# DMA time in a list schedule: a softmax attention and token-mixing MLP kernel planned again with DMA prices, finer DMA keys and measured GpSimd times

## The chip, the cores and the metric

The kernel runs on one core of one Trainium2 chip. The metric is device time in microseconds (us) of the whole program; each quoted time is the median of three to seven runs. A profile shows one further view, the span from first to last instruction, which is about 2 us shorter than the timed run. The core has TensorE (PE, matmuls), VectorE (DVE), ScalarE (ACT), GpSimd (POOL) and SyncE, whose sequencer (SPq) issues nearly all DMAs here. Every run also gives the mean granted clock of TensorE; that clock is either 1.0 or 0.5 at any moment, so a mean clock c over a span means 2 × (1 − c) × span microseconds "at half clock".

## The reference, cut to what matters

```python
x  = A_x                                 # 2048 x 512, bf16
xn = layernorm(x)
q, k, v = split(xn @ wqkv)               # 32 heads of 16
p  = softmax(q k^T / 4)                  # 32 x 2048 x 2048 exponents
a  = (p v) @ wo
u  = gelu(layernorm(xn)^T w1 + b1)       # mixes tokens: 2048 -> 1376
y  = (u w2 + b2)^T                       # 1376 -> 2048
return x + a + y
```

The exponents dominate: 134 million of them, cut into 1024 tiles of 128 × 1024. One tile is two heads' scores for part of the keys. Most tiles go to ScalarE (one instruction each); some go to VectorE, which approximates the exponent by integer arithmetic on the bits in five instructions (`dW`, `dM`, `dA`, square, product), and whose result needs three second matmuls instead of one.

## The kernel before

The kernel is written as a *list schedule*. A Python class places one instruction after another on the engine where it can start soonest, by a price list, and keeps a modelled clock for each engine. The chip then executes each engine's list in order, waiting on semaphores. Prices decide the order only; data dependencies are found by keys that each instruction reads and writes, in the order in which the instructions are planned. So a wrong price should give no wrong result, as long as no buffer is planned to be filled again before its reader is planned. What a wrong price does is to put an instruction where its engine must stand and wait.

```python
EXP_I, EXP_L = 0.903, 1.03      # ScalarE exponent: issue, latency (us)
P1_I, P1_L = 1.13, 1.22         # VectorE: first step of an exponent tile
DMA_L = 2.2                     # DMA: issue to landing
D_GAP = 3                       # at least so many tiles between two on VectorE
D_BACKLOG = 1.2                 # and no more VectorE work than this waiting
...
def _time(self, op, cost, ready):
    if op.is_dma:
        op.t0 = max(self.free[eng], ready)
        self.free[eng] = op.t0 + 0.06          # issue price of a DMA
        op.t1 = op.t0 + cost[1]                # 2.2
...
def task_qt(qb, T):                            # queries of a pair of head blocks
    ...
    for e_ in range(2):
        slot = (8 * qb + 2 * T + e_) % 4
        for r in range(4):
            a = 32 * r + 16 * e_
            yield "sp", [dict(dst=QT[a:a + 16, slot, :], src=Qall[a:a + 16, :], reads=[("Qall",)],
                              writes=[("QT", slot)], name="q_row")]     # one key for four rows
...
def task_epilogue(b):                          # head block b: divide by the row sums
    yield "pvev", [... tensor_copy(OT32[:, eb, :], bank(PV_BANK)) ...]          # VectorE
    for r in range(4):
        yield "sp", [... dcomp <- OT32 ...]                # 4 DMAs: row sums, reshaped
    yield "dve", [... reciprocal(rcomp, dcomp) ...]        # waits for these 4
    yield "sp", [... rden_d <- rcomp ...]                  # 1 DMA to DRAM
    for r in range(4):
        yield "sp", [... denb <- rden_d, broadcast ...]    # 4 DMAs back
    yield "dve", [... oT = OT32 * denb ...]                # waits for these 4
...
# GpSimd: normalisation of a row block and V scaling, both priced 0.9 us
def ln2_norm(t):  sc.add("pool", ..., cost=(0.9, 1.0))
def vm_scale(tiles, T):  sc.add("pool", ..., cost=(0.9, 1.0))
```

DMA generators (`yield "sp"`) were emitted at once when their turn came. The kernel works through 32 head blocks (four heads and 512 queries each) of 32 exponent tiles each; where the text below speaks of "a head" of the plan, it means such a block. Beside them it fills TensorE's spare time with "filler" tasks on one more PSUM bank: K, V and query projections, the MLP's up-projection (`ut`), and the output tiles (`fin`). Filler is unevenly spread: blocks 1 to 12 have 100 to 268 filler matmuls, blocks 13 to 16 and 20 to 24 have 0 to 16.

The softmax here doesn't subtract the row's maximum and nothing guards it: scores larger than these inputs give would overflow.

Of the kernel before, what the change touches and what calls it, by code (L numbers as in the profile page):

```python
# [11 lines left out]
F32 = mybir.dt.float32  # L12
# [44 lines left out]
DMA_L = 2.2  # L57
D_GAP = 3
D_LAST = 28
D_BACKLOG = 1.2  # L60
# [23 lines left out]
class Sched:  # L84
# [43 lines left out]
    def _time(self, op, cost, ready):  # L128
        eng = op.eng
        if op.is_dma:  # L130
            op.t0 = max(self.free[eng], ready)
            self.free[eng] = op.t0 + 0.06
# [22 lines left out]
    def add(self, eng, fn, reads=(), writes=(), name="", dma=False, out_dma=False, cost=None):  # L155
# [3 lines left out]
        if cost is None:  # L159
            cost = (0.06, DMA_L) if dma else (("F", (0, 1, 2, 3), 0.22) if eng == "pe" else (EV_I, EV_L))  # L160
# [94 lines left out]
def bass_parallel_sum__softmax_full_mha__mixer_token_mlp__prompt_kernel(  # L255
# [18 lines left out]
    with ExitStack() as es:  # L274
# [42 lines left out]
        u_sb = sb("u_sb", [128, 512], F32)  # L317
        ga_sb = sb("ga_sb", [128, 512], F32)
# [57 lines left out]
        sc.add("pool", lambda e: e.memset(QT[:, 2:4, :], 0.0), writes=[("QT", 2), ("QT", 3)], cost=(0.8, 0.9))  # L376
# [38 lines left out]
        def late_consts():  # L415
            for half in range(2):
                sc.add("pool", lambda e, half=half: e.memset(wo_pad[:, 4 * half:4 * half + 4, :], 0.0),
                       writes=[("wo_pad", g) for g in range(4 * half, 4 * half + 4)], cost=(1.8, 1.9))
            for e_ in range(2):
                for r in range(4):  # L420
                    src = A_wo.rearrange("(T q) n -> q T n", q=128)[32 * r + 16 * e_:32 * r + 16 * e_ + 16, :, :]
                    dst = wo_pad[32 * r:32 * r + 16, :, :].rearrange("p (T e) n -> p T e n", e=2)[:, :, e_, :]
                    dma("sp", dst, src, reads=[], writes=[("wo_pad", g) for g in range(NG)], name="ld_wo")
# [30 lines left out]
        def ln2_norm(t):  # L454
            sc.add("pool", lambda e: e.tensor_scalar(xn_sb[:, t, :], xn_sb[:, t, :], mv[:, t, 3:4], None, ALU.mult),  # L455
                   reads=[("xn", t), ("mv", t)], writes=[("xn", t)], cost=(0.9, 1.0))
# [49 lines left out]
        def vm_scale(tiles, T):  # L506
# [4 lines left out]
                cost=(0.9, 1.0))  # L511
# [17 lines left out]
        def qt0_evac():  # L529
            sc.add("act", lambda e: e.activation(QT[:, 0, :], bank(EX_BANK), ACTF.Identity, scale=qmask[:, 0:1]),  # L530
                   reads=[("bank", EX_BANK), ("qmask",)], writes=[("QT", 0)], cost=(0.6, 0.69))
            sc.add("dve", lambda e: e.tensor_scalar(QT[:, 1, :], bank(EX_BANK), qmask[:, 1:2], None, ALU.mult),
                   reads=[("bank", EX_BANK), ("qmask",)], writes=[("QT", 1)])
# [51 lines left out]
        def score_specs(n):  # L585
# [3 lines left out]
            for i in range(2):  # L589
# [6 lines left out]
                    reads=[("KTt", T, kt), ("QT", b % 4)], writes=[("bank", bk)], name="sc",  # L596
# [102 lines left out]
        def task_qt(qb, T):  # L699
            for ct in range(NCT):  # L700
# [5 lines left out]
                              reads=[("bank", EX_BANK)], writes=[("Qall",)])]  # L706
            for e_ in range(2):
                slot = (8 * qb + 2 * T + e_) % 4
                for r in range(4):
                    a = 32 * r + 16 * e_  # L710
                    yield "sp", [dict(dst=QT[a:a + 16, slot, :], src=Qall[a:a + 16, :], reads=[("Qall",)],
                                      writes=[("QT", slot)], name="q_row")]
# [32 lines left out]
        def w1_load(ft):  # L745
# [3 lines left out]
                reads=[], writes=[("wblk", slot)], name="ld_w1")  # L749

        def w2_load(i):
# [3 lines left out]
                reads=[], writes=[("wblk", slot)], name="ld_w2a")  # L755
            dma("sp", wblk[0:FLAST, slot, NFT - 1, :], B_w2[128 * (NFT - 1):F, 128 * st:128 * (st + 1)],
                reads=[], writes=[("wblk", slot)], name="ld_w2b")
            dma("sp", wblk[FLAST:FLAST + 1, slot, NFT - 1, :],
                B_b2[128 * st:128 * (st + 1)].rearrange("(o j) -> o j", o=1),
                reads=[], writes=[("wblk", slot)], name="ld_b2")  # L760
# [3 lines left out]
        def task_ut(ft):  # L764
            slot = ft % NW
            m = min(128, F - 128 * ft)
            for st in range(NT):
                yield "pe", ext_mm(m, lambda a, z, st=st: wblk[:, slot, st, a:z], xn_sb[:, st, :],
                                   [("wblk", slot), ("h", st)], st == 0, st == NT - 1, "ut")
            if ft + NW < NFT:  # L770
                yield "call", lambda: w1_load(ft + NW)
            else:
                yield "call", lambda: w2_load((ft + NW - NFT + 1) % 2 if NFT % 2 else ft + NW - NFT)
            yield "ev", [dict(eng="dve", fn=lambda e: e.tensor_scalar(u_sb[0:m, :], bank(EX_BANK)[0:m, :],  # L774
                                                                      b1col[0:m, ft:ft + 1], None, ALU.add),
                              reads=[("bank", EX_BANK), ("b1col",)], writes=[("u",)])]
            yield "free", None
            yield "dve", [dict(eng="dve", fn=lambda e: e.scalar_tensor_tensor(
                ga_sb[0:m, :], u_sb[0:m, :], GELU_A, u_sb[0:m, :], ALU.mult, ALU.mult),
                reads=[("u",)], writes=[("ga",)])]  # L780
            yield "dve", [dict(eng="dve", fn=lambda e: e.scalar_tensor_tensor(
                ga_sb[0:m, :], ga_sb[0:m, :], 1.0, u_sb[0:m, :], ALU.add, ALU.mult),
                reads=[("ga",), ("u",)], writes=[("ga",)])]
            yield "act", [dict(eng="act", fn=lambda e: e.activation(ga_sb[0:m, :], ga_sb[0:m, :], ACTF.Tanh, scale=GELU_C),
                               reads=[("ga",)], writes=[("ga",)], cost=(0.5, 0.64))]
            yield "dve", [dict(eng="dve", fn=lambda e: e.scalar_tensor_tensor(
                gT(ft)[0:m, :], ga_sb[0:m, :], 1.0, u_sb[0:m, :], ALU.add, ALU.mult),
                reads=[("ga",), ("u",)], writes=[("gT", ft)] + (WKV_KEYS if ft < 8 else []))]

        def task_fin(i):  # L790
# [5 lines left out]
            for ft in range(NFT):  # L796
                k = 128 if ft < NFT - 1 else FLAST + 1
                yield "pe", ext_mm(128, lambda a, z, ft=ft, k=k: wblk[0:k, slot, ft, a:z], gT(ft)[0:k, :],
                                   [("wblk", slot), ("gT", ft)] + ([("gTone",)] if ft == NFT - 1 else []),
# [3 lines left out]
            for G in range(ng):  # L803
                yield "pe", ext_mm(128, lambda a, z, G=G: oT[:, qb % 2, G, 128 * sti + a:128 * sti + z], wo_pad[:, G, :],
                                   [("oTc", qb % 2, G), ("wo_pad", G)], False, G == ng - 1, "op")
# [5 lines left out]
            else:  # L811
# [3 lines left out]
                    reads=[("bank", EX_BANK), ("x", st)], writes=[("osb", ob)])]  # L815
                yield "sp", [dict(dst=out2[128 * st:128 * (st + 1), :], src=osb[:, ob, :], reads=[("osb", ob)],
# [4 lines left out]
        def task_epilogue(b):  # L821
            qb, G = divmod(b, NG)
            eb = b % 2
            yield "pvev", [dict(eng="dve", fn=lambda e: e.tensor_copy(OT32[:, eb, :], bank(PV_BANK)),  # L824
# [9 lines left out]
            for r in range(4):  # L834
                yield "sp", [dict(dst=denb[32 * r:32 * r + 16, eb, :],
                                  src=rden_d[eb:eb + 1, 512 * r:512 * (r + 1)].to_broadcast([16, 512]),
                                  reads=[("rden_d", eb)], writes=[("denb", eb, r)], name="den_out")]
# [64 lines left out]
        for j in range(4):  # L902
            vm_scale(list(range(4 * j, 4 * j + 4)), 0)
# [321 lines left out]
```

## Time and profile before

The median was 879.62 us of three runs (873.07 to 880.71).

| | before |
|---|---|
| busy share: TensorE / VectorE / ScalarE | 90% / 83% / 90% |
| exponent tiles on ScalarE / VectorE | 839 / 185 |
| start to start of two ScalarE exponents when nothing stalls | 0.90 us |
| VectorE waits for the row-sum DMAs and the broadcast DMAs | 24.8 + 10.1 us |
| mean granted clock | 0.939 |

The next fence holds lines of the profile's page of the kernel before: the busy sums; the busy tenths of TensorE and ScalarE in 40 equal slices with the granted clock in tenths under them; and the engines on the chain that ended last.

```profile
PE 787.1 (90%) x8124; PEld 229.7 (26%) x8124; DVE 730.6 (83%) x1227; ACT 792.9 (90%) x860; POOL 78.5 (9%) x90
...
PE   5985899899999998999799999989989999898994
...
ACT  4984799899999998999989999998999999899992
...
PEclk9998899999999998989958999995899999999998
...
DVE 35%; PE 34%; DMA 13%; ACT 7%; SPq 5%; POOL 5%; issue 2%; DVEq 0%
```

Three engines are nearly equally busy, and 18% of the chain of waits is DMA or the DMA queue, though all DMA engines together are hardly used (29 GB/s). The clock row dips to 5 where ScalarE dips too.

The next fence cuts the same execution into stretches (view by windows): before the first exponent; block 0; block 1; blocks 2 to 4; 5 to 12; 13 to 31; after the start of the last exponent (below just "after the last exponent"). Block borders are every 32nd exponent start, read from the trace. Columns: from:to, length, busy us (and count) of PE, weight loads, DVE, ACT, POOL; granted clock; DMA share; GB/s.

```profile
0.00:16.60 16.60, 7.43 (x67) 6.44 (x67) 9.07 (x28) 5.36 (x10) 9.04 (x31) 1.00 0.78 221
16.60:48.30 31.70, 27.97 (x273) 13.82 (x277) 22.65 (x70) 29.77 (x32) 16.40 (x26) 0.89 0.01 2
48.30:88.50 40.20, 27.98 (x424) 8.82 (x424) 27.35 (x40) 24.81 (x27) 37.04 (x26) 0.85 0.22 46
88.50:169.20 80.70, 72.71 (x1216) 26.50 (x1216) 72.48 (x114) 73.50 (x79) 15.97 (x9) 0.97 0.05 11
169.20:377.90 208.70, 198.29 (x2232) 54.62 (x2232) 181.10 (x297) 201.45 (x224) 0.00 (x0) 0.98 0.21 44
377.90:859.00 481.10, 445.37 (x3840) 116.91 (x3842) 409.11 (x666) 456.95 (x490) 0.00 (x0) 0.93 0.08 19
859.00:876.30 17.30, 7.31 (x88) 2.62 (x80) 8.85 (x15) 1.02 (x2) 0.00 (x0) 0.77 0.09 30
```

Block 1 took 40.2 us with ScalarE busy 27.9 of them. Nineteen blocks (13 to 31) took 481 us, 25.3 us each, at clock 0.93. A block whose 26 ScalarE tiles follow each other at 0.90 us would take 23.5 us.

Who waited for whom (columns: engine and line, releaser, us in all, times, longest), first the engines, then the DMA queue's own:

```profile
DVE dW L619 <- PE ps L592: 65.6, 55, 4.7
...
ACT pT L608 <- PE ps L592: 52.6, 65, 6.0
...
DVE rcomp L830 <- DMA dcomp<-OT: 24.8, 18, 3.4
...
PE ps L654 <- POOL VM L508: 12.7, 5, 5.9
...
DVE oT L838 <- DMA denb<-rden_scratch: 10.1, 11, 2.4
```

```profile
SPq L348 <- DMA QT<-Qall: 121.6, 90, 3.0
...
SPq L348 <- DMA wblk<-in_B_w_dram: 75.1, 32, 3.9
```

The DMA queue stood 121.6 us behind query rows: four rows shared one key, so each waited for the landing of the one before.

### The profile page before, as it was taken

How to read it: one execution, taken by the hardware profiler on the slowest of the kernel's cores; microseconds unless marked ns; L12 is line 12 of the kernel's file. 1: busy time of each engine (PE TensorE's matmuls, PEld its weight loads, DVE VectorE, ACT ScalarE, POOL GpSimd, SP SyncE). 2: the span in 40 equal slices, each digit the busy share in tenths (PEclk: the TensorE clock that was granted, in tenths of full speed). 3: DMA queues.
4: the chain of work that ended last, by engine and by line, in shares of the span. 5: the costliest groups of instructions: out<-in, count | busy, mean ns of one | idle time of the engine just before them, and what ended most of it. 6: DMA issues, size and time to landing. Idle time of an engine off the chain costs nothing.

```text
span 876.3 us, 19148 instructions
## 1 busy us (share of the span) xinstructions
PE 787.1 (90%) x8124; PEld 229.7 (26%) x8124; DVE 730.6 (83%) x1227; ACT 792.9 (90%) x860; POOL 78.5 (9%) x90
## 2 busy tenths in 40 slices
PE   5985899899999998999799999989989999898994
PEld 3522333222222221222212222221222222222221
DVE  6775898898998877887868889897998888798985
ACT  4984799899999998999989999998999999899992
POOL 5499121100000000000000000000000000000000
PEclk9998899999999998989958999995899999999998
DMA  5003000022132102100000111100000111100110
GB/s 168 1 23 59 14 9 16 6 59 56 31 62 46 44 15 52 47 14 10 13 6 8 36 30 24 38 15 5 10 12 6 32 25 34 37 15 8 24 25 25
DMA packets 73238, 25.36 MB, mean 29 GB/s; under 512 B 63104, under 2 KB 71168, under 8 KB 73152
## 3 DMA queue, kind: packets, MB, share of 16 engines
q1 hardware_dynamic: 69984, 22.57, 11.4%
q10 hardware_dynamic: 3168, 1.57, 0.6%
q8 instruction: 63, 1.03, 0.5%
q14 instruction: 23, 0.19, 0.1%
HBM read 19.54 MB, written 2.35 MB: 25 GB/s over the span
## 4 chain that ended last, share of the span: by engine, by line
DVE 35%; PE 34%; DMA 13%; ACT 7%; SPq 5%; POOL 5%; issue 2%; DVEq 0%
PE ps L592 13%; DVE dW L619 13%; PE ps L654 12%; PE ps L683 7%; ACT pT L608 7%; DVE dM L630 5%; SPq L348 5%; DVE dM L628 5%; DMA dcomp<-OT 4%; DVE dM L622 4%; POOL hx L455 3%; DMA wblk<-in_B_w_dram 3%; DVE dA L625 2%; DMA denb<-rden_scratch 2%; DMA rden_scratch<-rcomp 2%
## 5 line engine op out<-in xcount | busy, mean ns | idle before, releaser
L608 ACT ACTIVATE pT<-ps 128x1024 bf16<-128x1024 f32 x839 | 783.7, 1098 | 55.4 <-PE ps L592 52.6
L592 PE MATMUL ps<-QT,KT 32*128 32x512 bf16 x2048 | 348.2, 403 | 35.3 <-DVE dW L619 21.3
L619 DVE TENSOR_SCALAR dW<-ps 128x1024 int16<-128x1024 f32 x185 | 225.6, 1219 | 66.2 <-PE ps L592 65.6
L654 PE MATMUL ps<-pT,V 128*32 128x512 bf16 x1678 | 274.2, 407 | 5.3 <-DVE OT L824 3.5
L592 PEld LDWEIGHTS ps<-QT,KT 32*128 32x128 bf16 x2048 | 85.2, 91 | 348.4 <-ACT pT L608 127.4
L630 DVE TENSOR_TENSOR dM<-dW,dM 128x1024 bf16<-128x1024 bf16 x185 | 127.7, 691 | 2.8
L628 DVE TENSOR_TENSOR dM<-dM 128x1024 bf16<-128x1024 bf16 x185 | 128.5, 695 | 0.0
L654 PEld LDWEIGHTS ps<-pT,V 128*32 128x32 bf16 x1678 | 64.5, 95 | 114.6 <-issue 89.1
L654 PE MATMUL ps<-dM,VM 128*32 128x512 bf16 x370 | 74.8, 408 | 16.1 <-POOL VM L508 12.7
L622 DVE TENSOR_SCALAR dM<-dW 128x1024 int16<-128x1024 int16 x185 | 80.7, 436 | 3.1
L654 PE MATMUL ps<-dW,V 128*32 128x512 bf16 x370 | 75.4, 411 | 8.7 <-DVE OT L824 7.9
L625 DVE TENSOR_SCALAR dA<-dW 128x1024 int16<-128x1024 int16 x185 | 78.6, 425 | 0.0
L654 PE MATMUL ps<-dA,V 128*32 128x512 bf16 x370 | 73.6, 410 | 1.0 <-DVE V L740 0.5
L683 PE MATMUL ps<-hx,wblk 128*32 128x512 bf16 x688 | 57.8, 383 | 0.3 <-DVE u_sb L774 0.3
L683 PE MATMUL ps<-wkv_raw,wblk 128*32 128x512 bf16 x512 | 41.4, 383 | 1.8 <-DVE Qall L705 1.2
L683 PE MATMUL ps<-wo_pad,oT 128*32 128x512 bf16 x480 | 42.0, 392 | 0.0
L508 POOL TENSOR_SCALAR VM<-V 128x544 bf16<-128x544 bf16 x16 | 26.9, 1685 | 65.2 <-DVE V L740 62.3
L838 DVE TENSOR_TENSOR oT<-OT,denb 128x512 bf16<-128x512 f32 x31 | 21.3, 688 | 10.1 <-DMA denb<-rden_scratch 10.1
L830 DVE RECIPROCAL rcomp<-dcomp 128x16 f32<-128x16 f32 x31 | 7.8, 252 | 24.9 <-DMA dcomp<-OT 24.8
L654 PEld LDWEIGHTS ps<-dM,VM 128*32 128x32 bf16 x370 | 18.1, 96 | 38.7 <-issue 15.3
L455 POOL TENSOR_SCALAR hx<-hx,mv 128x512 bf16<-128x512 bf16 x16 | 26.7, 1684 | 0.1
L654 PEld LDWEIGHTS ps<-dW,V 128*32 128x32 bf16 x370 | 17.9, 95 | 32.2 <-issue 14.7
(79 smaller groups left out, 373.4 us busy)
## 6 DMA issues: line engine op xcount, KB each, us to landing
wblk<-in_B_w_dram SPq DMA_DIRECT2D x10, 512.0 KB, 4.4
wblk<-in_B_w_dram SPq DMA_DIRECT2D x16, 320.0 KB
denb<-rden_scratch SPq DMA_DIRECT2D x124, 32.0 KB, 1.8
out_dram<-osb SPq DMA_DIRECT2D x16, 128.0 KB, 1.8
dcomp<-OT SPq DMA_DIRECT2D x124, 2.0 KB, 1.7
QT<-Qall SPq DMA_DIRECT2D x120, 16.0 KB, 1.7
x_sb<-in_A_x_dram SPq DMA_DIRECT2D x3, 512.0 KB, 10.1
wkv_raw<-in_A_wqkv_dram ACTq DMA_DIRECT2D x2, 384.0 KB, 9.4
```

The lines of the kernel that those rows point to most:

```text
L348: return eng.dma_start(dst, src)
L455: sc.add("pool", lambda e: e.tensor_scalar(xn_sb[:, t, :], xn_sb[:, t, :], mv[:, t, 3:4], None, ALU.mult), reads=[("xn", t), ("mv", t)], w ...
L508: sc.add("pool", lambda e: e.tensor_scalar(vm_kh[:, t0_:t0_ + n, 8 * T:8 * T + 8, :], v17_kh[:, t0_:t0_ + n, 8 * T:8 * T + 8, :], CM, None ...
L592: specs.append(dict(eng="pe", fn=lambda e, r=r, bk=bk: e.matmul(bank(bk), lhsT=KT[32 * r:32 * r + 32, T, 128 * kt:128 * (kt + 1)], rhs=QT[ ...
L608: return [dict(eng="act", fn=lambda e: e.activation(pT[:, pbuf[n], :], ps[:, s_ * 1024:(s_ + 1) * 1024], ACTF.Exp, scale=LN2_128), reads=[ ...
L619: yield dict(eng="dve", fn=lambda e: e.tensor_scalar(dW_i[:, buf, :], ps[:, s_ * 1024:(s_ + 1) * 1024], IBIAS, 0.0, ALU.add, ALU.max), rea ...
L622: yield dict(eng="dve", fn=lambda e: e.tensor_scalar(dM_i[:, buf, :], dW_i[:, buf, :], 0x7f, 0x3f80, ALU.bitwise_and, ALU.bitwise_or), rea ...
L625: yield dict(eng="dve", fn=lambda e: e.tensor_scalar(dA_i[:, buf, :], dW_i[:, buf, :], -128, None, ALU.bitwise_and), reads=[("dW", buf)], ...
L628: yield dict(eng="dve", fn=lambda e: e.tensor_tensor(dM[:, buf, :], dM[:, buf, :], dM[:, buf, :], ALU.mult), reads=[("dM", buf)], writes=[ ...
L630: yield dict(eng="dve", fn=lambda e: e.tensor_tensor(dM[:, buf, :], dW[:, buf, :], dM[:, buf, :], ALU.mult), reads=[("dW", buf), ("dM", bu ...
L654: specs.append(dict(eng="pe", fn=lambda e, r=r, off=off, i=i: e.matmul(bank(PV_BANK)[32 * r:32 * r + 32, :], lhsT=vt[:, off:off + 32], rhs ...
L683: specs.append(dict(eng="pe", fn=lambda e, c=c, w=w: e.matmul(bank(EX_BANK)[32 * c:32 * c + w, :], lhsT=lhs_of(32 * c, 32 * c + w), rhs=rh ...
```

## The change

The intent: give the schedule true prices for DMAs and GpSimd, and let DMAs take part in it, so that no engine is made to stand in front of a transfer that has not landed. Five parts:

```diff
-DMA_L = 2.2            D_GAP = 3      D_BACKLOG = 1.2       # issue price was 0.06
+DMA_I = 0.6
+DMA_L = 3.5            D_GAP = 4      D_BACKLOG = 1.6
...
# 1. DMAs are candidates of the list schedule, not emitted at once; "gates" keep a
#    buffer until its reader is planned
-                if kind == "sp":
-                    for w in what:
-                        dma("sp", ...)
-                    continue
+            for g in frees:
+                if g["cur"] and g["cur"][0] == "sp":
+                    cands.append((max(sc.free["sp"], sc.ready("sp", ..., dma=True)), 0, "dma", g))
...
+            yield "gate", lambda: b < 2 or b - 2 in oT_done         # in task_epilogue
# 2. finer keys: a row, a part of a weight block, one of eight parts of wo_pad
-                                      writes=[("QT", slot)], name="q_row")]
+                                      writes=[("QT", slot, r)], name="q_row")]
-                reads=[], writes=[("wblk", slot)], name="ld_w2b")
+                reads=[], writes=[("wblk", slot, "b")], name="ld_w2b")
# 3. GpSimd: measured prices, first V scalings during block 0, wo_pad cleared by VectorE
-                   reads=[("xn", t), ("mv", t)], writes=[("xn", t)], cost=(0.9, 1.0))
+                   reads=[("xn", t), ("mv", t)], writes=[("xn", t)], cost=(1.65, 1.75))
-                cost=(0.9, 1.0))
+                cost=(1.6, 1.7))
...
# 4. the gelu's u and ga get two buffers; K and V fall due earlier
-        u_sb = sb("u_sb", [128, 512], F32)
+        u_sb = sb("u_sb", [128, 2, 512], F32)
-        KV_DUE = {1: BN + 8, 2: 2 * BN + 24, 3: 4 * BN}
+        KV_DUE = {1: BN + 2, 2: 2 * BN + 16, 3: 3 * BN + 24}
# 5. the last output tiles begin 54 tiles earlier and wait, head by head, at gates
-                rel = BN * (NBLK - 2) + 14
+                rel = BN * (NBLK - 2) + FIN_REL          # FIN_REL = -40
+                yield "gate", lambda G=G: 8 * qb + G in oT_done
```

The new plan puts 200 tiles on VectorE in place of 185.

## The prediction

> **What bounds it now.** ScalarE (90% busy), TensorE (90%) and VectorE (83%) are nearly balanced (busy table). Of 1024 exponent tiles, 839 run on ScalarE and 185 on VectorE (groups of instructions). In the trace, ScalarE starts follow each other every 0.90 us when nothing stalls. So 32 head blocks of 32 tiles, 26 of them on ScalarE, need 23.5 us each; the blocks took 23.1 to 40.2 us. Summed over the kernel the stall beyond 0.90 us is about 75 us. The rest is 17 us before the first exponent and 17 us after the last.
>
> Where the stall sits (windows of 22 us): 66–110 us has ScalarE busy only 10.4 and 17.5 of 22 us; there TensorE waited on the GpSimd scaling of V (12.7 us in the waits, up to 5.9 at once) behind long GpSimd normalisations of 1.68 us, which the old schedule priced at 0.9. Further, VectorE waited 24.8 us for the denominator DMAs and 10.1 us for the broadcast ones, in order, holding up score slots. The DMA queue itself waited 121.6 us for earlier query-row DMAs and 75.1 us for weight DMAs: rows under one dependency key landed one after the other, 1.7 us each. The chain of waits has DMA 13%, its queue 5%, GpSimd 5%. Two blocks near 450 and 605 us took 31 and 30 us at a granted clock of half, with little filler matmul work.
>
> **What the change does** (instruction order of both kernels):
> - 200 instead of 185 tiles go to VectorE: 15 × 0.90 = 13 us less ScalarE, 15 × about 3.1 = 47 us more VectorE, 60 more small matmuls.
> - Reciprocal and normalising multiply of a head now stand two or three VectorE tiles later, so the 35 us of DMA waits should nearly vanish.
> - Query-row and weight DMAs no longer wait for each other.
> - The wo_pad clear moves from GpSimd (3.5 us) to VectorE, V scaling of the first heads goes into block 0, and later scalings queue behind at most about one normalisation.
> - Two u/ga buffers let the next up-projection overlap the gelu.
> - Last output tiles: 64 instead of 68 filler matmuls still stand after the last score, so the tail gains about nothing.
>
> **Cost on the critical path.** Estimates from these durations: block 1 from 40 to about 29 us, blocks 2–4 −3, blocks 5–12 −10 (DMA waits), lighter blocks −16 (about 13 from moving tiles), tail 0. Sum about −42 us. Not all of the 35 us of VectorE waits pays, since ScalarE ran on during part of them; and VectorE becomes the equal of ScalarE, about 24 us per block.
>
> **Predicted:** 836 us, 80% range 816 to 856. Faster by over 2%: 0.93; same 0.06; slower 0.01.
>
> **What the profile would show.** VectorE waits for the denominator and broadcast DMAs under 8 us together (was 35); TensorE waits for GpSimd under 4 us (was 12.7); queue waits on query rows near zero; 824 ScalarE exponents of the same 1.1 us; VectorE busy share near 90%; block 1 under 31 us; the stretch after the last exponent still 16–17 us.
>
> **What would make it wrong.** The clock. The Trainium skill, "TensorE: Matmul & The Clock Gate" (The HAM clock gate), says the gate halves the clock by how busy TensorE recently was; this trace shows about 110 us at half clock, mostly in stretches without filler work, and blocks there cost 6 us more. If filler work is more clustered, more such blocks come and eat 10–20 us; if denser scores avoid them, the result is nearer 820. Second, the schedule still prices a multiply on VectorE at 0.60 where some took 0.72, so a VectorE loaded with 200 tiles may fall behind the plan and hold score slots. Third, an output tile that waits for its heads keeps the filler bank.

## The result, and the profile after

The changed kernel took 813.9 us (median of four runs, 812.6 to 815.71); the kernel before 880.16 us in the same rounds. The ratio is 0.9257, 95% interval 0.9194 to 0.9319. Ratios here are the mean time of one kernel's fast runs over that of the other's of the same rounds, so not quite the ratio of the quoted medians. The direction was right, the size was not: 813.9 lies below the stated range of 816 to 856.

The same lines of the changed kernel's page:

```profile
PE 754.5 (93%) x8184; PEld 230.1 (28%) x8184; DVE 764.3 (94%) x1304; ACT 771.7 (95%) x845; POOL 76.8 (9%) x88
...
PE   5988999999999999999999999899899999999995
...
ACT  4998999999999999999999999999999999899991
...
PEclk9999999999999999999899999999999999799998
...
ACT 43%; DVE 31%; PE 24%; DMA 1%; issue 1%; SPq 0%; DVEq 0%
```

ScalarE and VectorE are now 95% and 94% busy, the clock row has two dips left between start and end, and DMA is 1% of the chain.

The same stretches of the changed kernel:

```profile
0.00:15.50 15.50, 7.25 (x67) 6.26 (x67) 8.91 (x28) 5.37 (x10) 9.06 (x31) 1.00 0.83 237
15.50:47.10 31.60, 27.95 (x273) 13.75 (x277) 24.16 (x72) 29.74 (x32) 16.19 (x29) 0.89 0.14 30
47.10:75.80 28.70, 23.50 (x412) 8.61 (x414) 27.75 (x41) 24.67 (x27) 25.00 (x15) 1.00 0.19 36
75.80:150.30 74.50, 69.59 (x1248) 24.73 (x1244) 74.15 (x119) 72.42 (x79) 26.58 (x15) 1.00 0.05 11
150.30:346.80 196.50, 194.61 (x2200) 55.24 (x2200) 188.70 (x314) 195.99 (x220) 0.00 (x0) 1.00 0.22 46
346.80:795.90 449.10, 423.91 (x3920) 118.73 (x3922) 431.12 (x719) 442.47 (x481) 0.00 (x0) 0.98 0.09 21
795.90:813.60 17.70, 7.65 (x88) 2.80 (x80) 9.53 (x17) 1.00 (x2) 0.00 (x0) 0.78 0.09 31
```

Its waits; VectorE's waits for row-sum and broadcast DMAs are gone altogether, and the DMA queue no longer waits for query rows or weights:

```profile
DVE dW L617 <- PE ps L590: 21.9, 20, 2.7
...
ACT pT L606 <- PE ps L590: 14.6, 27, 2.2
...
PE ps L652 <- POOL VM L506: 1.3, 1, 1.3
```

Against the prediction, in us (block borders as above; the profiled runs):

| stretch | before | after | change | predicted |
|---|---|---|---|---|
| to the first exponent, block 0 | 16.6 + 31.7 | 15.5 + 31.6 | −1.2 | 0 |
| block 1 | 40.2 | 28.7 | −11.5 | −11 |
| blocks 2 to 4 | 80.7 | 74.5 | −6.2 | −3 |
| blocks 5 to 12 | 208.7 | 196.5 | −12.2 | −10 |
| blocks 13 to 31 | 481.1 | 449.1 | −32.0 | −16 |
| after the last exponent | 17.3 | 17.7 | +0.4 | 0 |
| span | 876.3 | 813.6 | −62.7 | about −42 |

So most of the miss, 16 of 21 us, sits in blocks 13 to 31. (The predicted terms add up to 40; the prediction has "about −42".)

How such a block loses its time is best read from one place in the kernel before, the start of block 15 (timeline; columns: start, length, engine, line, operation; in brackets the idle time before it and what ended it):

```profile
430.57 0.68 DVE L824 COPY OT<-ps 128x512 f32<-128x512 f32 x1
...
431.28 2.43 SPq L348 DMA_DIRECT2D dcomp<-OT  x4
...
434.98 0.39 PE L592 MATMUL ps<-QT,KT 32*128 32x512 bf16 x2
...
436.47 0.25 DVE L830 RECIPROCAL rcomp<-dcomp 128x16 f32<-128x16 f32 x1 [2.74 <-DMA dcomp<-OT]
436.64 1.16 DVE L619 TENSOR_SCALAR dW<-ps 128x1024 int16<-128x1024 f32 x1
...
437.86 0.39 PE L592 MATMUL ps<-QT,KT 32*128 32x512 bf16 x2 [2.17 <-DVE dW L619]
...
438.58 0.61 PE L592 MATMUL ps<-QT,KT 32*128 32x512 bf16 x4
```

VectorE copies the block's result at 430.57. The four row-sum DMAs take 2.43 us to issue and the last has landed 5.2 us after the first was issued. (The Trainium skill, "Perfetto Trace Analysis", DMA Instruction — HWDGE, says that the profiled window of a DMA instruction leaves out the movement of the data; here the 2.43 us are indeed only the issue.) The old plan had priced this at 3 × 0.06 + 2.2 = 2.4 us and put the reciprocal there, so VectorE stood still for 2.74 us. The next exponent tile on VectorE was late, its PSUM slot stayed taken, and TensorE stood still for 2.17 us before the next score matmuls. At 438.4 the granted clock then fell to half (clock records of the trace): the score matmuls go from 0.39 to 0.61 us in the last two lines. It stayed there for 20 us, and block 15 took 31.4 us. The new price, 3 × 0.6 + 3.5 = 5.3 us, covers this place, which is one of the slowest: before the 18 reciprocals that had to wait, the time from the first issue to the start of the reciprocal was 3.5 to 5.3 us, 3.6 at the median. So the old price was over a microsecond too low at all 18, and the new one is that of the slowest. In the changed kernel the reciprocal of a head stands later, behind more VectorE work, and needs no wait:

```profile
306.09 0.68 DVE L829 COPY OT<-ps 128x512 f32<-128x512 f32 x1
...
307.86 2.42 SPq L349 DMA_DIRECT2D dcomp<-OT  x4
...
313.51 0.24 DVE L835 RECIPROCAL rcomp<-dcomp 128x16 f32<-128x16 f32 x1
```

### The profile page after: what moved, and what is told of

It is laid out like the page before. It is cut to its first block, busy times and chain, and to the rows that moved or that the text cites. A ratio compares the mean times of both kernels' runs of the same rounds, so it can differ in the third digit from the quotient of the medians.

```text
span 813.6 us, 19375 instructions
## 1 busy us (share of the span) xinstructions
PE 754.5 (93%) x8184; PEld 230.1 (28%) x8184; DVE 764.3 (94%) x1304; ACT 771.7 (95%) x845; POOL 76.8 (9%) x88
## 4 chain that ended last, share of the span: by engine, by line
ACT 43%; DVE 31%; PE 24%; DMA 1%; issue 1%; SPq 0%; DVEq 0%
ACT pT L606 42%; DVE dW L617 10%; PE ps L590 9%; PE ps L652 7%; PE ps L681 7%; DVE dM L626 5%; DVE dM L628 4%; DVE dM L620 3%; DVE dA L623 2%; DVE OT L829 1%; DVE V L739 1%; DVE KT L720 1%; DMA x_sb<-in_A_x_dram 1%; DVE oT L844 1%; PE ps L478 0%
## 5 line engine op out<-in xcount | busy, mean ns | idle before, releaser
L606 ACT ACTIVATE pT<-ps 128x1024 bf16<-128x1024 f32 x824 | 763.2, 1113 | 15.4 <-PE ps L590 14.6
L590 PE MATMUL ps<-QT,KT 32*128 32x512 bf16 x2048 | 331.5, 390 | 23.3 <-ACT pT L606 10.7
L652 PE MATMUL ps<-pT,V 128*32 128x512 bf16 x1648 | 259.0, 393 | 7.2 <-DVE OT L829 3.3
L617 DVE TENSOR_SCALAR dW<-ps 128x1024 int16<-128x1024 f32 x200 | 243.4, 1217 | 23.0 <-PE ps L590 21.9
L628 DVE TENSOR_TENSOR dM<-dW,dM 128x1024 bf16<-128x1024 bf16 x200 | 137.0, 685 | 1.7
L626 DVE TENSOR_TENSOR dM<-dM 128x1024 bf16<-128x1024 bf16 x200 | 137.6, 688 | 0.0
L620 DVE TENSOR_SCALAR dM<-dW 128x1024 int16<-128x1024 int16 x200 | 86.5, 433 | 1.6
L623 DVE TENSOR_SCALAR dA<-dW 128x1024 int16<-128x1024 int16 x200 | 85.0, 425 | 0.0
L506 POOL TENSOR_SCALAR VM<-V 128x544 bf16<-128x544 bf16 x16 | 29.0, 1811 | 47.6 <-DVE V L739 42.1
L652 PEld LDWEIGHTS ps<-dA,V 128*32 128x32 bf16 x400 | 19.4, 95 | 20.7 <-issue 9.7
L829 DVE COPY OT<-ps 128x512 f32<-128x512 f32 x31 | 21.2, 683 | 1.1 <-PE ps L652 0.7
```

Source lines behind the costliest of these rows:

```text
L506: sc.add("pool", lambda e: e.tensor_scalar(vm_kh[:, t0_:t0_ + n, 8 * T:8 * T + 8, :], v17_kh[:, t0_:t0_ + n, 8 * T:8 * T + 8, :], CM, None ...
L590: specs.append(dict(eng="pe", fn=lambda e, r=r, bk=bk: e.matmul(bank(bk), lhsT=KT[32 * r:32 * r + 32, T, 128 * kt:128 * (kt + 1)], rhs=QT[ ...
L606: return [dict(eng="act", fn=lambda e: e.activation(pT[:, pbuf[n], :], ps[:, s_ * 1024:(s_ + 1) * 1024], ACTF.Exp, scale=LN2_128), reads=[ ...
L617: yield dict(eng="dve", fn=lambda e: e.tensor_scalar(dW_i[:, buf, :], ps[:, s_ * 1024:(s_ + 1) * 1024], IBIAS, 0.0, ALU.add, ALU.max), rea ...
L620: yield dict(eng="dve", fn=lambda e: e.tensor_scalar(dM_i[:, buf, :], dW_i[:, buf, :], 0x7f, 0x3f80, ALU.bitwise_and, ALU.bitwise_or), rea ...
L623: yield dict(eng="dve", fn=lambda e: e.tensor_scalar(dA_i[:, buf, :], dW_i[:, buf, :], -128, None, ALU.bitwise_and), reads=[("dW", buf)], ...
```

## The experiments

Theory A: VectorE's waits for DMAs and the stretches at half clock that they set off were most of the gain that I had not counted. Theory B: the 15 more tiles on VectorE (less ScalarE work) made the gain. Runs of one group were on the same chip, with the kernel before in the same rounds: a1 to a4 (without a3_keys_mended); b2, b4, s_light and s_rich; c_after, d_price, d_after and b3; d0_price, a5, a3_keys_mended and v_tail; d0_after and d0h_price. The times at half clock in the expectations (41 us for the changed kernel, 109 for the kernel before) were a first count; the clock records within the span give 35 and 107.

| run | what it is | median us | ratio to before | clock | blocks 13–31, us |
|---|---|---|---|---|---|
| a2_price | changed, old DMA prices | 871.02 | 0.9769 | 0.932 | 495.6 |
| a1_share | changed, old limits (186 tiles) | 828.84 | 0.9264 | 0.976 | 453.8 |
| a3_keys | changed, coarse keys (wrong result) | 853.17 | 0.9543 | 0.974 | 445.0 |
| a4_pool | changed, GpSimd part undone | 821.55 | 0.9183 | 0.983 | 444.9 |
| b2_price | before, new DMA prices (wrong result) | 900.16 | 1.0255 | 0.906 | 490.5 |
| b4_share | before, new limits (200 tiles) | 859.99 | 0.9818 | 0.960 | 457.0 |
| s_light | changed, six forced waits, light blocks | 844.11 | 0.9592 | 0.961 | 469.4 |
| s_rich | changed, six forced waits, filler-rich blocks | 829.30 | 0.9451 | 0.970 | 443.7 |
| c_after | changed, control | 814.29 | 0.9159 | 0.983 | 444.7 |
| d_price | a2_price + planned dummy matmuls | 835.27 | 0.9383 | 0.985 | 459.9 |
| d_after | changed + planned dummies | 812.85 | 0.9147 | 0.987 | 446.4 |
| b3_price_keys | before, new prices, fine keys, gates | 841.85 | 0.9462 | 0.973 | 448.2 |
| d0_price | a2_price + unplanned dummies | 880.92 | 0.9937 | 0.974 | 503.7 |
| a5_fin | changed, late start of last tiles | 819.44 | 0.9248 | 0.983 | 447.1 |
| a3_keys_mended | a3_keys + one gate (still wrong) | 857.16 | 0.9657 | 0.953 | 450.8 |
| v_tail | changed, last four tiles interleaved | 811.66 | 0.9167 | 0.982 | 444.7 |
| d0_after | changed + unplanned dummies | 853.35 | 0.9701 | 0.991 | 484.2 |
| d0h_price | a2_price + half as many | 867.68 | 0.9858 | 0.966 | 492.1 |

Clock and the last column are of the profiled run. The profiled run of a3_keys_mended is slow. The kernel before had medians of 898.3, 882.31, 892.87, 885.54 and 884.61 us in the five groups, on different chips, so its ratios differ by up to 2% from group to group; the changed kernel had 813.9 and 814.29 in two groups. A difference between runs of different groups therefore carries more doubt than its decimals say, above all for runs that, like the kernel before, spend long at half clock. a2_price, from which many differences below are taken, ran only in the group where the kernel before was slowest.

### Old DMA prices in the changed kernel (a2_price)

```diff
-DMA_I = 0.6
-DMA_L = 3.5
+DMA_I = 0.06
+DMA_L = 2.2
```

> The changed kernel with the two DMA prices of the schedule set back (issue 0.06 us, landing 2.2 us); 200 tiles stay on VectorE, all keys and GpSimd prices stay. In the plan, reciprocal and normalising multiply stand some 8 and 10 VectorE instructions after what they need, in place of 13 and 18. Theory A (VectorE waits for denominator DMAs, and the stretches at half clock that they set off, were most of the gain beyond my estimate): VectorE waits for DMAs come back to 20 to 35 us, time at half clock rises well above the 41 us of the changed kernel, 835 to 850 us in all. Theory B (the 15 more tiles on VectorE, that is less ScalarE work, made the gain): under 822 us, light blocks stay at 23.0 to 23.5 us.

Measured: 871.02 us. Two constants, with 200 tiles still on VectorE and everything else kept, cost 57 us (by the ratios to the kernel before, 0.9769 against 0.9257, about 45 us), more than theory A had expected and far outside theory B. VectorE's waits are back, and blocks 13 to 31 ran at clock 0.90 (waits, then the stretch of blocks 13 to 31):

```profile
DVE oT L844 <- DMA denb<-rden_scratch: 28.6, 14, 4.2
...
DVE rcomp L835 <- DMA dcomp<-OT: 8.6, 7, 3.2
```

```profile
357.50:853.10 495.60, 447.30 (x3912) 117.95 (x3912) 431.29 (x712) 450.56 (x481) 0.00 (x0) 0.90 0.08 18
```

From its clock records the run spent 102 us at half clock between the first and the last exponent (leaving out the first 10 us); the changed kernel 20 us, its control 14 us, the kernel before 92 us. Theory B falls as an explanation of the main gain.

### Old limits in the changed kernel (a1_share)

```diff
-D_GAP = 4              D_BACKLOG = 1.6
+D_GAP = 3              D_BACKLOG = 1.2
```

> The changed kernel with the old limits on VectorE tiles: 186 tiles on VectorE, 838 on ScalarE, all else kept. Theory A: the price of 14 tiles on ScalarE at 0.90 us, about +13 us, 823 to 829 us, clock as before, no DMA waits. Theory B: more than that, 835 us or above, because ScalarE binds every block.

Measured: 828.84 us, 15 us more, at an unchanged clock and with 0.5 us of waits for broadcast DMAs. That is the price of 14 more ScalarE tiles (12.7 us) and little else, as theory A had it. So once the waits are gone, tiles are worth what they cost on ScalarE. The run says one thing more. Counted in the traces, it has 118 tiles on VectorE in blocks 13 to 31, exactly as many as the kernel before (the changed kernel has 128), and yet these blocks took 453.8 us in place of 481.1: 27 us went without a tile moved there. The stretch:

```profile
372.20:826.00 453.80, 417.80 (x3803) 118.66 (x3802) 401.75 (x654) 433.77 (x472) 0.00 (x0) 0.97 0.09 21
```

### Coarse keys (a3_keys, a3_keys_mended)

```diff
-    writes=[("QT", slot, r)], name="q_row"
+    writes=[("QT", slot, z) for z in range(4)], name="q_row"
     # and so for the parts of wblk and wo_pad
```

> The changed kernel with coarse dependency keys for query rows, second weights and output weights (each DMA waits for the one before it to land); the schedule knows of it, and puts 203 tiles on VectorE. Theory A says the plan moves what depends on them away, so VectorE waits stay under 8 us but score starts come late at every second head: 820 to 835 us, DMA queue waits for query rows back near 120 us. If fine keys alone were the gain: 845 us or above. If they did nothing: within 3 us of 814.

> The coarse-key run with a gate that keeps the query buffer until its eight rows are planned (the earlier run overwrote it and gave a wrong result). Fine keys matter most where a head needs its query rows soon after they are made, in block 1: block 1 takes 45 us or more in place of 29, the other blocks stay within 1 us, 835 to 855 us in all. If the earlier 853 us came from the error itself: under 825 us.

Both gave a wrong result; the first time lies above the 820 to 835 us of theory A, the second just above its 835 to 855, and the queue's waits for query rows came to 40.8 us in the first, not to 120. My guess for the second, an overwritten query buffer, was wrong: its error was the same. An assertion in the planner, which needs no chip, then found the cause: with coarse keys the planned DMA queue runs so late that an output buffer is filled again before its store is planned, and that output is lost (planned again without a chip, it happens twice in both runs and never in the changed kernel); the changed kernel has no gate there because it does not need one. Instructions, sizes and waits are otherwise those of a correct run, but a price of the keys from these two runs is only an indication: block 1 took 47.6 and 50.0 us in place of 28.7, block 9 took 45.7 in the first (25.4 in the changed kernel), and blocks 13 to 31 took as little as in the changed kernel in the first. That would fit a plan that moves everything away from slow DMAs, except where a head cannot start without its query rows; it is argued, not shown.

### GpSimd part undone (a4_pool)

```diff
-    cost=(1.65, 1.75))   # normalisation        -    cost=(1.6, 1.7))   # V scaling
+    cost=(0.9, 1.0))                            +    cost=(0.9, 1.0))
-    wo_pad cleared on VectorE in block 0, first V scalings in block 0
+    wo_pad cleared on GpSimd after block 0, first V scalings after block 0
```

> The changed kernel with the GpSimd part undone: normalisation and V scaling priced at 0.9 us again, output-weight clear on GpSimd (3.5 us), first V scalings after block 0. Both theories: the loss is confined to blocks 1 to 3, which together took 78.5 us and will take 88 to 96; TensorE waits for GpSimd come back to about 10 to 20 us; 824 to 832 us in all. If it costs more than 20 us, the stall has set off half clock elsewhere.

Measured: 821.55 us, 7 us more. Blocks 1 to 3 took 34.5 + 26.9 + 24.6 = 86.0 us in place of 78.5, and TensorE waited 8.7 us for the V scaling (1.3 in the changed kernel). The place was right, the size somewhat under what was expected. (The Trainium skill, "GPSIMD Engine Reference", section 3.1, has GpSimd 1.96 times as slow as VectorE on an fp32 addition of two tensors. No run here repeats that operation. The clear of `wo_pad` took 3.5 us on GpSimd in the kernel before and 2 × 0.91 us on VectorE in the changed one, but there with half as many elements of twice the size. On one shape, 128 × 512 bf16 to bf16 with per-row factors, the kernel before has 1.68 us on GpSimd (L455) and 0.41 us on VectorE (L439), a factor of four.)

### The parts on the kernel before (b2_price, b4_share, b3_price_keys)

```diff
 # b2_price
-DMA_L = 2.2             # issue 0.06
+DMA_I = 0.6
+DMA_L = 3.5
 # b4_share
-D_GAP = 3               D_BACKLOG = 1.2
+D_GAP = 4               D_BACKLOG = 1.6
 # b3_price_keys: b2_price, and
-    writes=[("QT", slot)]          writes=[("wblk", slot)]
+    writes=[("QT", slot, r)]       writes=[("wblk", slot, "a")]   # "b", "c"
+    yield "gate", lambda: b < 2 or b - 2 in oT_done               # in task_epilogue
```

> The kernel before with the DMA prices alone (issue 0.6 us, landing 3.5 us); coarse keys, old GpSimd prices, old limits; the plan puts 192 tiles on VectorE. Theory A (DMA waits of VectorE and the half clock that they set off): VectorE waits for DMAs fall from 35 to under 12 us, time at half clock falls from 109 us to under 70, 845 to 860 us. Theory B (number of tiles on VectorE): 7 tiles times 0.90, so 872 to 876 us.

> The kernel before with the new limits alone: 200 tiles on VectorE instead of 185. Theory A: VectorE still waits 30 us or more for DMAs and the clock still drops, 868 to 882 us. Theory B: 15 times 0.90 us less ScalarE, 867 us or below, and light blocks near 23.3 us.

> The kernel before with the DMA prices, fine keys for query rows and weights, and a gate that keeps a head's row buffer until its multiply is planned (without it the earlier run of the prices alone overwrote that buffer and gave a wrong result); old GpSimd prices and old limits, 190 tiles on VectorE. Theory A: VectorE waits for DMAs under 8 us, time at half clock under 60 us, light blocks 23.5 to 24.5 us, 838 to 852 us. Rival (tile share or GpSimd was the gain): 865 us or above.

b2_price was slower (900.16 us) and wrong: the same kind of assertion showed that the plan five times refills a head's result buffer before the multiply of two heads earlier is planned, which is what the change's gate forbids. Its plan also has a price that the change avoids: each of four query rows on one key is now planned to land 3.5 us after the one before, and block 1 took 58.6 us. In this kernel at least, true prices without fine keys were no gain.

b3_price_keys is right and took 841.85 us, as theory A expected: no VectorE waits for row-sum or broadcast DMAs, and blocks 13 to 31 at 448.2 us, the changed kernel's level, with 190 tiles on VectorE and the old GpSimd prices. What it lacks of the changed kernel is mostly in block 1 (49.1 us against 28.7). Its light blocks fell by 33 us with 120 tiles on VectorE there, two more than before. It has neither the DMAs as candidates nor the second u/ga buffer, so neither is needed for that gain; their own worth was not tested.

b4_share took 859.99 us. That is below what theory A expected (868 to 882) and inside what theory B expected for the total, though its light blocks did not reach B's 23.3 us (457.0 / 19 = 24.1). Its trace shows why it cannot decide: VectorE's waits for DMAs had fallen from 35 to 20 us (16.9 + 3.0) and half clock from 92 to 51 us, because the new limits shifted the plan. The limits alone were worth some 2% (ratio 0.9818, 95% interval 0.973 to 0.9907), partly through waits and clock.

### Forced waits (s_light, s_rich)

```diff
 # the changed kernel, denominator DMAs of six heads b in SET at a false price
-    writes=[("dcomp", eb, r)], name="den_in")]
+    writes=[("dcomp", eb, r)], name="den_in", cost=(0.0, 0.1) if b in SET else None)]
 # s_light: SET = (13, 14, 19, 20, 21, 22)     s_rich: SET = (4, 5, 6, 7, 8, 9)
```

> The changed kernel with one false price: the denominator DMAs of six heads (13, 14, 19 to 22, all followed by blocks with little filler matmul work) are priced at 0.1 us, so the plan puts their reciprocal early and VectorE really waits, some 2 to 3 us each, 12 to 18 us together. Theory A with a clock that multiplies: time at half clock rises by 30 us or more, and the kernel loses more than the waits themselves, +15 to +30 us. Rival (a wait costs at most itself, the clock falls on its own where filler is thin): half clock stays near 41 us, +4 to +12 us.

> The same false price on six heads (4 to 9) followed by blocks full of filler matmul work. Theory A: TensorE keeps busy through the wait, the clock stays at full, and the kernel loses no more than the waits: +4 to +12 us. If the clock has nothing to do with filler work, the same loss and half clock as in the run with light blocks.

Real waits of 13.4 us (light) and 11.4 us (rich) came about. s_light: median 844.11 us, 30 above the control (which ran on another chip); its profiled run was its fastest at 835.5, with 51 us at half clock against 14 to 20, all of it in blocks 15, 20, 21 and 23, where forced waits fell. s_rich: 829.3 us, 15 above, with 17 us at half clock in the blocks of the waits. The medians mix in other things: s_light's profiled run, from which the waits are read, was its fastest and s_rich's its slowest, and block 1, before any forced wait, took 28.7 and 34.0 us, so some 5 us of s_rich are not the waits'. Cleaner is the stretch with the waits in the profiled runs. Blocks 13 to 31 of s_light took 20 to 25 us more than in the two profiles of the changed kernel (469.4 against 449.1 and 444.7), 1.5 to 1.8 us for each us of wait. Blocks 5 to 12 of s_rich took 15.6 us more (212.1 against 196.5), 1.4 us for each. So in both a wait cost more than itself; that it costs clearly more where filler is thin is not shown. My expectation that filler would keep the clock at full was too strong: 17 us of half clock came in filler-rich blocks as well.

### Is the clock a cause or a companion?

First without an experiment. The kernel before was run 35 times beside the others, on five chips. The program was the same each time, the mean clock not: 26 fast runs had spans of 869.5 (clock 0.956) to 896.5 us (clock 0.902). A straight line through these 26 is

span = 848.4 us + 0.27 × (us at half clock), correlation 0.98.

All 35, the slow ones too, give 846.6 and 0.28. One and the same block of the changed kernel says the same: block 28 took 28.4 us in the first profile, with 13.7 us at half clock, and 23.7 us in the control's, with none; the instructions are the same (0.34 us per us). That is a relation within one program, not yet an intervention: it does not tell whether half clock makes the run longer or something else makes both. So I tried to hold the clock by giving TensorE useless work.

```diff
 # d_price (on a2_price) and d_after (on the changed kernel): low-priority filler tasks in 12 light blocks
+        def task_dummy(n0):
+            for q in range(2):
+                yield "pe", ext_mm(128, lambda a, z: wq_sb[:, 0, a:z], xnT[:, 0, 0:512], ..., True, True, "dummy")
 # d0_price, d0_after, d0h_price: emitted beside the second matmuls, at no cost to the plan
+                if pv_block in LIGHT and cur_ext is None:       # d0h: every other time
+                    keep = (sc.free["pe"], sc.pe_end, ...)
+                    for s_ in ext_mm(... "dummy"): add(s_)
+                    sc.free["pe"], sc.pe_end, ... = keep
```

> The changed kernel itself, unedited, as a control on the same chip as the next three: about 814 us, 812 to 820, clock 0.975 to 0.985, if it depends on the chip as little as its own four runs did. The kernel before spread from 871 to 914 us over the runs so far.

> The run with the two old DMA prices (871 us, 102 us at half clock, VectorE waiting 37 us for DMAs) plus dummy matmuls: in the 12 blocks with little filler work, up to 24 groups of four matmuls whose result nobody reads, put only where the plan has TensorE idle. The waits stay; TensorE does more work. Theory A2 (the clock is a cause: it falls because TensorE does too little, and then TensorE at half clock binds the block): time at half clock falls below 60 us and the kernel gets FASTER, 835 to 855 us, though nothing useful was added. Rival (the low clock only accompanies the waits, which are the cost): same time or slower, 868 to 885 us.

> The changed kernel plus the same dummy matmuls in the blocks with little filler work (198 tiles on VectorE in the plan, 826 on ScalarE). Theory A2: the 20 us at half clock after the first block vanish, blocks 15 and 28 fall from 25.1 and 28.4 to about 23.3 us: 806 to 811 us, a version faster than both. Rival: 814 us or slower, by the work added.

d_price, with more work for TensorE, was 36 us faster than a2_price: 835.27 us, 10 us at half clock. The gain lies where the dummies are: blocks 13 to 31 fell from 495.6 to 459.9 us, blocks 5 to 12, without dummies, stayed (207.5 and 207.4). But the plan took the dummies into account, moved two tiles to ScalarE, and VectorE's DMA waits in blocks 13 to 31 fell as well, from 27 to 12 us. Clock and waits were not separated. d_after showed nothing to gain any more: 812.85 us against the control's 814.29, where 806 to 811 had been expected.

> The run with old DMA prices plus dummy matmuls that the plan does not see: the order of instructions on VectorE, ScalarE, GpSimd and the DMA queue is the same as in that run, instruction for instruction; only TensorE does more. If the clock is a cause: half clock in blocks 13 to 31 falls from about 92 us to under 30, these blocks from 496 to 455 to 475 us, though VectorE still waits 20 us or more for DMAs in them; the other blocks do not change. If the earlier dummy run gained by its plan and not by its clock: these blocks stay at 490 us or above.

> The changed kernel plus the unplanned dummies, every other engine's order unchanged. If the dummies cost what the clock gave back in the run with old prices: blocks 13 to 31 rise from 445 to 449 us to 465 us or above, 832 to 850 us in all, at a clock as high as the control's. If the dummies are free, and the clock is no cause: 811 to 818 us.

> Old DMA prices with about half as many unplanned dummies (56 to 92 matmuls in a block with little filler work, as many as the filler-rich blocks have). If half clock costs about 0.3 us for each us of it (what same-program runs of different clock show) and dummies cost in proportion: half clock falls to 30 to 60 us, VectorE still waits 25 us or more for DMAs, 850 to 866 us, faster than the 871 us without dummies. If the clock is no cause: 870 us or above.

In d0_price the order on all other engines was that of a2_price, instruction for instruction. It held the clock (17 us at half clock in blocks 13 to 31 in place of 99), yet took 880.92 us; my expectation failed. Taken alone that speaks against the clock. The control d0_after says why it doesn't: the same dummies, unplanned, stand before score matmuls and cost the changed kernel 39.5 us in blocks 13 to 31 (444.7 to 484.2), at full clock throughout (853.35 us in all, slightly more than expected). In d0_price the same dummies cost only 8 us there (495.6 to 503.7). The missing 31 us are what the clock may have given back, together with dummies that lay inside waits and so cost nothing, and with DMA waits of VectorE there that fell from 27 to 22 us. 82 us less half clock at 0.27 would be 22 us, an estimate from the line above. Half as many dummies (d0h_price) gave 867.68 us, between the two expectations. That is 3 us less than a2_price, but by the ratios of the two groups it is slower (0.9858 against 0.9769), so it decides nothing. The stretch of blocks 13 to 31 in d0_price and in d0_after:

```profile
360.70:864.40 503.70, 476.27 (x5294) 137.99 (x5293) 433.68 (x712) 455.63 (x481) 0.00 (x0) 0.98 0.08 18
```

```profile
348.10:832.40 484.30, 471.07 (x5289) 138.74 (x5290) 434.86 (x719) 452.49 (x481) 0.00 (x0) 1.00 0.08 20
```

So the clock's cost is supported from three sides (same program at different clocks, one block with and without, the dummies' balance), the first two near 0.3 us per us at half clock, but no run changed the clock and nothing else, and the third compares runs of different groups. One rival can be set aside: the changed kernel did not keep its clock by spreading filler, for in the trace each of the two kernels has 11 of the blocks 13 to 31 with 24 filler matmuls or fewer.

### The last output tiles (a5_fin, v_tail)

```diff
 # a5_fin
-        FIN_REL = -40
+        FIN_REL = 14        # and no start before all heads are normalised
 # v_tail: VectorE order in the tail, r = reciprocal + multiply, s = final add (waits for TensorE)
-        r0 s0 r1 s1 r2 s2 r3 s3
+        r0 r1 s0 r2 s1 r3 s2 s3
```

> The changed kernel with the last output tiles starting as before (after their heads are normalised, 54 tiles later). My prediction said that the early start gains about nothing: 811 to 818 us. If the early start hides filler work: 820 us or above, by a longer tail after the last exponent than 17.7 us.

> The changed kernel with the last four output tiles interleaved on VectorE: reciprocal and multiply of the next quarter stand before the final add of this one, which waits for TensorE. The add waits 0.5 to 0.7 us for TensorE three times, so 1.5 to 2 us less: tail 15.7 to 16.2 us in place of 17.7, 811 to 813 us against 814.

a5_fin took 819.44 us; after the last exponent 21.7 us passed in place of 17.7. It lies between the two expectations: the early start is worth 4 us of tail in the new plan. v_tail took 811.66 us (809.93 to 813.38), the lowest median of all though not clear of d_after's 812.85, ratio 0.9167 to before. It was not run on the same chip as a control of the changed kernel; what it gained is read from the end of the two profiles. Two of the four final adds of the changed kernel, each after a wait for TensorE:

```profile
803.16 0.69 DVE L876 SCALAR_TENSOR_TENSOR osb<-ps,hx 128x512 bf16<-128x512 f32 x1 [0.48 <-PE ps L871]
...
808.10 0.69 DVE L876 SCALAR_TENSOR_TENSOR osb<-ps,hx 128x512 bf16<-128x512 f32 x1 [0.70 <-PE ps L871]
```

and two of v_tail, without:

```profile
800.43 0.68 DVE L878 SCALAR_TENSOR_TENSOR osb<-ps,hx 128x512 bf16<-128x512 f32 x1
...
802.22 0.68 DVE L878 SCALAR_TENSOR_TENSOR osb<-ps,hx 128x512 bf16<-128x512 f32 x1
```

The stretch after the last exponent took 15.2 us in place of 17.7.

## Why the prediction was wrong

**Right.** *What bounds it*, *where the stall sits* and *what the change does* held. VectorE waits for DMAs: predicted under 8 us, measured none. TensorE waits for GpSimd under 4: 1.3 (TensorE's matmuls; 1.9 for its weight loads). Queue waits for query rows: none. 824 exponents of 1.1 us: 1113 ns. Block 1 under 31 us: 28.7. VectorE near 90%: 94%. The stretch after the last exponent: 17.7 us, just over the 16 to 17 predicted.

**Wrong: the size of one term, the light blocks.** The step reads "lighter blocks −16 (about 13 from moving tiles)". It leaves some 3 us there for the DMA waits and nothing for the clock; blocks 13 to 31 gave −32.0. Both parts of the split failed. Moving tiles was put too high: only 10 of the 15 moved tiles lie in these blocks, an estimated 9 us at 0.90, and between a1_share and the two profiles of the changed kernel they are worth 5 to 9 us (453.8 against 449.1 and 444.7). The waits were put far too low: VectorE's DMA waits in blocks 13 to 31 were 19.9 us (14.5 + 5.4), and with the half clock beside them they cost 27 us (a1_share, no tile moved there) to 31 us (b3_price_keys, 33 less two tiles).

The prediction had read the half clock ("Two blocks near 450 and 605 us took 31 and 30 us at a granted clock of half") and the DMA waits, and kept them apart: the waits went into the sum, the clock into *What would make it wrong*, as something that could go either way. In the runs they came together. Two DMA prices alone brought 37 us of waits and 82 us more of half clock back and cost 45 to 57 us (a2_price); forced waits of 11 to 13 us cost 16 to 25 in their own blocks. How much is the clock's is an estimate: in blocks 13 to 31, half clock fell from 68 to 20 us, which at 0.27 per us is 13 us of the 32. That the other 19 are near the 16 that I had put is chance, since mine were mostly tiles. For the whole span: 107 us at half clock before, 36 after (from the mean clocks 0.939 and 0.978), 71 × 0.27 = 19 us, and 62.7 − 19 = 44, where my sum had 42; the same caution holds. The estimate takes the slope within the kernel before as holding between the two kernels.

**Right, with a footnote.** *Tail 0*: +0.4 us against the kernel before. But the early start was not idle: without it the tail of the new plan would be 4 us longer (a5_fin).

**Not borne out.** That 13 of the 16 us came from moving tiles. a1_share shows 15 us for 14 tiles over the whole kernel once waits are gone, but 5 to 9 of them in blocks 13 to 31; b4_share, the same limits on the kernel before, changed waits and clock with them.

**Open.** How a loss divides between a wait and the half clock that follows it, for one wait; and what exactly makes the clock fall (below). The price of fine keys in a correct kernel with true prices was not measured, since both runs of it lost output tiles; nor was that of the DMAs as candidates or of the second u/ga buffer.

## What to carry to other kernels

Where a static schedule orders the engines, a price that is too low makes an engine stand in front of the transfer; here that was worse than one that is too high (the new price of 5.3 us lies above the usual 3.6 and left no wait). Measure first issue to last landing of the whole group of DMAs, not one landing (here 3.6 us at the median of the waits and up to 5.3, against a price of 2.4), and give the group keys that do not chain its members. When such a wait also starves TensorE, count its length and then the half clock that may follow; regressing time on the mean clock over repeated runs of one program gives an estimate of what that is worth before anything is changed. And check a split such as "13 from moving tiles" stage by stage: a count of tiles per block in the two plans would have shown that a third of them lie elsewhere.

## What the Trainium skill lacked or had wrong

- "TensorE: Matmul & The Clock Gate" (HAM oscillation — how this bites in real kernels) gives "no PE-idle gaps >~3.4µs" as the abstract rule. Its next section, on a second failure mode, has the clock fall on frequent shorter pauses as well, but gives no figure for them. The clock fell after far shorter gaps than the rule's: in the 6.8 us before the falls at 438.4 and 592.0 us of the kernel before, the longest idle time of TensorE was 2.17 and 0.99 us, and before the fall at 699.9 us of the changed kernel 0.20 us; at none of the falls of these two traces had TensorE paused for more than 3.2 us in the 6.8 us before it. Few matmuls went with these three falls: 36, 40 and 42 recorded in 6.8 us, against 80 and 62 in an ordinary stretch of each kernel (some records can be missing). That is no rule either: at 380.4 us of the kernel before the clock fell after 68 matmuls and no pause over 0.51 us, and it stayed at full after other stretches with 42 or fewer, as after the 39 before 793.4 us. What makes it fall stays open. The fences below show busy times and counts in such windows, first two windows before a fall and an ordinary one of the kernel before, then one before a fall and an ordinary one of the changed kernel.

```profile
431.60:438.40 6.80, 4.20 (x36) 1.20 (x34) 4.02 (x8) 4.80 (x6) 0.00 (x0) 1.00 0.05 6
585.20:592.00 6.80, 4.99 (x40) 1.37 (x38) 4.84 (x9) 6.39 (x8) 0.00 (x0) 1.00 0.07 10
500.00:506.80 6.80, 6.55 (x80) 1.73 (x78) 6.73 (x12) 6.80 (x8) 0.00 (x0) 1.00 0.07 23
```

```profile
693.10:699.90 6.80, 6.16 (x42) 1.82 (x40) 5.05 (x10) 6.80 (x9) 0.00 (x0) 1.00 0.00 0
560.00:566.80 6.80, 6.19 (x62) 1.99 (x60) 6.70 (x13) 6.78 (x9) 0.00 (x0) 1.00 0.04 6
```

- The same page (The HAM clock gate) has the clock either half or full and its window 3413 ns. All clock records are 1.0 or 0.5, and every fall that ends before the last instruction lasts a whole multiple of 3.4 us, from 3.4 to 37.5. No page says what a microsecond at half clock costs a kernel that is bound by other engines as well: here 0.27 us goes with it (a line through 26 runs of one program, no proof of cause), while score matmuls go from 0.39 to 0.61 us.
- "DMA: Bandwidth & Descriptors" (Latency and other measured facts) speaks of a DMA fixed cost of about 2 us. For one DMA this case is near it (1.7 us from issue to landing at the median for the 2 KB row sums). No page has the price of a group on one queue: four such DMAs took 2.4 us to issue at the median, and where a reciprocal had to wait for them, 3.6 us at the median of 18 from the first issue to its start (5.2 us in the place shown).
